# Last block's chunks before its sums, shared normalising, a third own room, and two sums moved to POOL, in an adaLN block with linear attention and an MLP

## The chip, the cores and the metric

The kernel runs on one core of one Trainium2 chip. The metric is the device time of one execution in microseconds (us); the times shown are the median of three runs, beside one profiled execution. The engines are TensorE (PE: matmuls; PEld: its weight loads), VectorE (DVE), ScalarE (ACT), GpSimd (POOL) and SyncE (SP, whose in-order queue issues all DMAs of the main loops). Each engine works through its own instructions in order and waits on semaphores of the others.

## The reference

The input has 2048 tokens of width D = 576. `mod` gives six rows of D: shift, scale and gate for attention (sa, ca, ga) and for the MLP (sb, cb, gb).

```python
mod = (silu(c) @ w_mod).reshape(1, 6, 1, D)
h = layernorm(x) * (1 + ca) + sa
q, k, v = split(h @ wqkv)                  # 32 heads of 18
pq, pk = phi(q), phi(k)                    # phi(t) = where(t > 0, t + 1, exp(t)) + 1e-6
kv = einsum("bhsd,bhse->bhde", pk, v); z = sum_s(pk)
o = (pq @ kv) / (pq . z + 1e-6)
x = x + ga * (o @ wo)
h = layernorm(x) * (1 + cb) + sb
x = x + gb * (silu(h @ w1) @ w2)           # w1: 576 x 4608, w2: 4608 x 576
```

All is float32. Every large product is made from operands split into a high part (a cast to fp32r by ACT) and a low part (the rest, a subtraction on DVE or POOL), in three passes: high by high, high by low, low by high.

## The kernel before

Tokens stand in 16 tiles of 128 (acc, four blocks of 512 tokens). A first part makes the modulation, K and V and the sums over tokens. A second part (the loop over s, up to about 405 us) runs attention's output for tile t (attn_out, L580), the layer norm of its block (stats, finish, normalise), and, per block, a generator turn_all, which transposes the normalised block (turn_chunk_k: PE transposes into a PSUM bank "small", ACT modulates it, and high and low parts go to hT). The five chunks of 128 features are 0, 2, 4, 1, 3; chunk 4 is the tail of 64 (tail_h, tail32). Beside this, the first of 18 groups of 256 hidden features is done plainly: mlp_up (L641) and mlp_down (L655), called from a list named filler.

The other 17 groups (Weights and Unit) use seven products in Winograd's manner in place of eight: the two token blocks of a pair and the feature halves make a 2x2 scheme. Their operands are sums of chunks of two blocks: turn_all makes them for the odd block of each pair (blocks 1 and 3), out of the even block's chunks, kept in h32s ("H"), and the odd block's, in temporaries "sl" (two buffers): L729 to L734 are the sums, split_s (L688 and L62) makes S. Sums for the first pair are on POOL, for the second on DVE. With two sl buffers, chunk c and chunk 2+c are turned, summed and split before the next two are turned.

The operands n = 1 to 7 of both pairs go to DRAM (hd, L685); ten of the fourteen are fetched again for every group and pair (fetch, L917), in the order ORDER = 1, 6, 2, 5, 7, 3, 4. The first two fetches have rooms of their own (rooms0, "first"); the others go in turn to three rooms: halves of h2[3] and h2[2] (both named hT) and one "room". passes(n) issues the fetch of three operands further on once its matmuls are done.

A group's weights: load1 (L871) fetches w1's columns into raw, sums1 makes four sums on POOL (L862 to L865), and up(n) splits each (L883, L62). load2 (L889) fetches w2's rows into the same single raw buffer; sums2 multiplies them by gb (L893, DVE, 128x1152), makes four sums on POOL again, and split2 splits (L905, L62).

For each unit (one group, one pair) PE alternates between Unit.up (L941), the seven up products of this unit, and the fourteen down products (L1029) of the unit before. PE's order is written by hand; that of the other engines is a planner's. After an up product DVE adds into f (L958, L965, L979), ACT takes silu (L980), and operands1 and operands2 make the down operands: ha and hb (DVE), hd, hc and he (POOL: L999, L1005, L1007, L1010, with L990 for the low half). Every down product is added on DVE (L1033) from one of four PSUM banks in two buffers, to acc or to U[b], a sum that several outputs share. In the last group add_u (L1047) adds U to three quarters of each block, and the output is stored (L1052, L1070).

The order around the change is thus set by: the hand-written order on PE, the planner's order on DVE, ACT, POOL and SP, and the rooms (single or double buffers) that DMAs and engines wait for.

Of the kernel before, what the change touches and what calls it, by code (L numbers as in the profile page):

```python
# [8 lines left out]
F32 = mybir.dt.float32  # L9
F32R = mybir.dt.float32r  # L10
# [5 lines left out]
P = 128  # L16
# [5 lines left out]
def kernel(ctx: ExitStack, tc, A_x, A_wqkv, A_wo, B_x, B_w1, B_w2, c, w_mod, out):  # L22
# [8 lines left out]
    V, A, G, T = nc.vector, nc.scalar, nc.gpsimd, nc.tensor  # L31
# [15 lines left out]
    G2 = 2  # L47
    NG = F // (G2 * P)

    def f32(ap):  # L50
        return ap.bitcast(F32)
# [9 lines left out]
    def sub_hi(lo, full, hi):  # L61
        return V.tensor_sub(lo, full, f32(hi))  # L62
# [623 lines left out]

    def split_s(S, c, t):
        A.copy(S[:, c], t)  # L688
        sub_hi(S[:, 2 + c], t, S[:, c])

    def turn_chunk_k(tb, k, h32):
        ps = small()
        transpose_chunk(xn2[tb], k, ps)
        modulate(ps, k, None, cols["b"], h32, A)
        if k < KC:
            hi, lo = hpart(tb, k, 0), hpart(tb, k, 1)
            A.copy(hi, h32)
            sub_hi(lo, h32, hi)
        else:
            tail_h(htail(tb), h32)  # L700

    def turn_all(tb):

        nonlocal wqp, h2p, tail32, h32s
        if tb == 1:
            wqp.release()
            wqp = tc.alloc_tile_pool(name="hTb", bufs=1, side="right", reuse_waits="tile")
        if tb == 3:
            pb.release()
            h2p = tc.alloc_tile_pool(name="hTc", bufs=1, side="right", reuse_waits="tile")  # L710
        h2[tb] = hTa.tile([P, 2 * KC + 2, 512], F32R, name="hT")
        pair, eng = tb // 2, (G, V)[tb // 2]
        if tb % 2 == 0:
            h32s = pc.tile([P, KC, 512], F32, name="H")
            tail32 = pc.tile([P, 512], F32, name="ht")
            for k in CHUNKS:
                turn_chunk_k(tb, k, h32s[:, k] if k < KC else tail32)
                yield
        else:
            def temp():  # L720
                return pc.tile([P, 512], F32, name="sl", bufs=2)

            pool = wqp if pair == 0 else h2p
            S = [pool.tile([P, 4, 512], F32R, name="S", bufs=2) for _ in range(2)]
# [11 lines left out]
            t = temp()  # L736
            turn_chunk_k(tb, KC, t)
            G.tensor_sub(tail32, tail32, t)
            tail_h(h2[tb - 1][:, DIFF, :], tail32)
            yield  # L740
        up, down = mlp_units(tb, w)
        if tb < NB - 1:
            filler.extend(up + down)
        else:
            filler[:] = up + filler + down
        e, o = h2[tb - tb % 2], h2[tb]
        if tb % 2 == 0:
            store_h(pair, 1, e[:, 0:4, :])
            store_h(pair, 2, e[:, 4:9, :])
        else:  # L750
            for n, q in ((0, 5), (1, 6)):
                store_h(pair, q, S[n])
            store_h(pair, 5, o[:, 9:10, :], 4)
            store_h(pair, 4, o[:, ODD : ODD + 5, :])
            store_h(pair, 3, e[:, DIFF : DIFF + 1, :], 4)
            S = [wqp.tile([P, 4, 512], F32R, name="S", bufs=2) for _ in range(2)]
            for n, q in ((0, 7), (1, 3)):
                for c in range(2):
                    split_s(S[n], c, h32s[:, 2 * n + c])
                store_h(pair, q, S[n])  # L760
                hr[q] = S[n]
                yield
# [16 lines left out]
    while s < NT + 5 or filler or turns:  # L779
        if s < QB - 2:  # L780
            filler.append(late_q)
        if s == 4:
            w = load_mlp(0)
        if NP0 <= s < NT:
            prod = pb.tile([P, D], F32, name="prod")
            G.tensor_mul(prod, acc[s], z)
            pns[s] = q_norm(s, prod, pb.tile([P, DX], F32, name="pn", bufs=2))
        t = s - 2
        if t in (5, 9, 13, 17):
            turns.append(turn_all(t // 4 - 1))  # L790
# [55 lines left out]
    class Weights:  # L846
# [43 lines left out]

        def sums2(self):
            r2, t = self.r2, self.temps(HALF)
            V.tensor_mul(r2, r2, bc["gb"].unsqueeze(1).to_broadcast([P, G2, D]))  # L893
# [18 lines left out]
    def fetch(i):  # L912
        if i < len(streamed):
            _, q, n = streamed[i]
            room = rooms0[i] if i < 2 else rooms[(i - 2) % 3]
            m = hd[q, n].shape[1]
            nc.sync.dma_start(f32(room[:, :m, :]), hd[q, n])  # L917
            in_room[i] = room

    class Unit:  # L920
# [7 lines left out]
        def passes(self, n, ps, first, k=None):  # L928

            i = at.get((self.g, self.pair, n))  # L930
            if i is None:
                h, tail = hr[n], hr_tail.get(n)
            else:
                h = in_room.pop(i)
                tail = h[:, 4, :] if k is not None else None
            w, wt = self.w.w1[n], self.w.wt
            seq = [(w[:, b], h[:, a, :]) for c in range(2) for a, b in ((c, c), (c, 2 + c), (2 + c, c))]
            if k is not None:
                seq += [(wt[:, i, k * P : (k + 1) * P], tail) for i in range(2)]
            for m, (left, right) in enumerate(seq):  # L940
                T.matmul(ps, left, right, start=first and m == 0, stop=m == len(seq) - 1, skip_group_check=True)  # L941
            if i is not None and i >= 2:
                fetch(i + 3)

        def new_f(self, i, k):
# [48 lines left out]
        def operands1(self, i):  # L994

            half = self.half
            self.split(i, "ha", half(i, 0, 0), 1)
            s3 = pf.tile([P, 1, HT], F32, name="s3")
            G.tensor_sub(s3, half(i, 0, 0), half(i, 0, 1))  # L999
            self.split(i, "hd", s3, 7, eng=G)  # L1000

        def operands2(self, i):
            half = self.half
            s = pf.tile([P, 2, HT], F32, name="s")
            G.tensor_add(s[:, 0:1], half(i, 0, 1), half(i, 1, 1))  # L1005
            self.split(i, "hb", half(i, 1, 0, 2), 2, 4)
            G.tensor_sub(s[:, 1:2], s[:, 0:1], half(i, 0, 0))  # L1007
# [64 lines left out]
    with tc.manual_schedule(engines={mybir.EngineType.PE}):  # L1072
# [82 lines left out]
```

## Time and profile before

| what | value |
|---|---|
| median of 3 runs | 1214.83 us (1214.72 to 1222.22) |
| profiled execution | 1219.38 us, span 1217.3 us |
| granted TensorE clock, mean | 0.987 |
| PE busy | 1158.2 us (95%), PEld 1052.3 us (86%) |
| DVE busy | 979.5 us (80%) |
| POOL busy | 600.3 us (49%) |
| ACT busy | 523.9 us (43%) |
| DMA | 268.59 MB, mean 221 GB/s |
| down products, L1029, and up products, L941, in the chain that ended last | 21% each |

Busy time is the time in which an engine executes; waits on semaphores are not in it. The chain that ended last is followed back from the last instruction to what released it. Durations used further on come from this one profiled execution, whose clock starts at the span's first instruction.

### The profile page before, as it was taken

Reading aid. Unit: us, or ns where it says so; the run is one execution under the profiler, and the core shown is the slowest. Engines: PE = TensorE matmul, PEld = TensorE weight load, DVE = VectorE, ACT = ScalarE, POOL = GpSimd, SP = SyncE. Lnnn points to the kernel's source line nnn. Section 1 sums busy time; section 2 is a strip of 40 time slices with the busy share of each in tenths; the row PEclk is TensorE's granted clock in tenths of the full one; section 3 lists DMA queues with packets and bytes.
Section 4 is the critical chain, followed back from the end, with each engine's and each line's share of the span. In section 5 each row is a group of like instructions: output and inputs, shape, how many; then the busy total and the mean of one; then the engine's idle time right before and its main releaser. Section 6 shows DMA issues by size and latency. Waiting matters only on the chain.

```text
span 1217.3 us, 19338 instructions
## 1 busy us (share of the span) xinstructions
PE 1158.2 (95%) x7167; PEld 1052.3 (86%) x7167; DVE 979.5 (80%) x1583; ACT 523.9 (43%) x1067; POOL 600.3 (49%) x673
## 2 busy tenths in 40 slices
PE   5999999999988899999999999999999999999997
PEld 4999999899986688889889888888888888888887
DVE  6746754898858588898888898888898888888887
ACT  5434342315546444444344444344444444444431
POOL 3200000321402376676567567657757756766761
PEclk8999999999988999999999999999999999999999
DMA  9212300213243869769679679688687687697664
GB/s 284 86 40 88 113 1 1 67 44 122 96 194 134 348 262 340 266 239 334 257 248 357 251 262 341 232 305 308 252 317 287 250 328 280 251 340 268 237 249 146
DMA packets 57579, 268.59 MB, mean 221 GB/s; under 512 B 5450, under 2 KB 20046, under 8 KB 34446
## 3 DMA queue, kind: packets, MB, share of 16 engines
q1 hardware_dynamic: 57486, 267.36, 60.4%
q8 instruction: 57, 0.93, 0.3%
q14 instruction: 36, 0.29, 0.1%
HBM read 250.56 MB, written 16.78 MB: 220 GB/s over the span
## 4 chain that ended last, share of the span: by engine, by line
PE 62%; DVE 23%; issue 6%; DMA 5%; ACT 2%; POOL 2%; SPq 0%; DVEq 0%; POOLq 0%; ACTq 0%
PE down L1029 21%; PE up L941 21%; PE psK L154 10%; DVE w L62 5%; PE big L154 4%; DVE U L1033 3%; DVE acc L1033 3%; DMA raw<-in_B_w_dram 2%; DVE raw L893 2%; DVE hb L990 2%; DVE f L979 1%; DVE ha L990 1%; PE small L641 1%; PE kvp L390 1%; DMA hT<-hd 1%
## 5 line engine op out<-in xcount | busy, mean ns | idle before, releaser
L1033 DVE TENSOR_TENSOR acc<-down,acc 128x576 f32<-128x576 f32 x335 | 245.6, 747 | 17.2 <-PE down L1029 14.2
L941 PE MATMUL up<-hT,w 128*128 128x512 f32 x876 | 227.2, 394 | 4.6 <-DMA hT<-hd 4.6
L941 PEld LDWEIGHTS up<-hT,w 128*128 128x128 f32 x876 | 156.1, 188 | 31.2 <-DVE f L979 2.8
L1005 POOL TENSOR_TENSOR s<-f,f 128x256 f32<-128x256 f32 x67 | 52.1, 778 | 244.5 <-ACT f L980 244.5
L1029 PEld LDWEIGHTS down<-w,hb 128*128 128x128 f32 x804 | 114.4, 189 | 27.7 <-DVE U L1033 14.4
L1029 PE MATMUL down<-w,hb 128*128 128x288 f32 x804 | 126.9, 300 | 11.4 <-DVE U L1033 10.5
L1033 DVE TENSOR_TENSOR U<-down,U 128x576 f32<-128x576 f32 x134 | 100.6, 751 | 39.8 <-PE down L1029 39.1
L154 PE MATMUL psK<-w,hT 128*128 128x288 f32 (+2 forms) x896 | 128.6, 302 | 1.8 <-ACT hT L133 0.9
L154 PEld LDWEIGHTS psK<-w,hT 128*128 128x128 f32 x896 | 123.8, 193 | 3.1 <-DVE hT L62 1.7
L1029 PE MATMUL down<-w,hc 128*128 128x288 f32 x804 | 122.8, 295 | 0.6 <-DVE acc L1033 0.6
L1029 PEld LDWEIGHTS down<-w,hc 128*128 128x128 f32 x804 | 116.1, 189 | 6.9 <-issue 0.8
L989 ACT CAST hc<-s 128x512 fp32r<-128x512 f32 x67 | 41.7, 622 | 135.0 <-POOL s L1007 135.0
L990 POOL TENSOR_TENSOR hc<-s,hc 128x512 fp32r<-128x512 f32 x67 | 89.2, 1331 | 11.0 <-ACT hc L989 11.0
L980 ACT ACTIVATE f<-f 128x512 f32<-128x512 f32 x102 | 64.4, 631 | 54.8 <-DVE f L979 54.5
L941 PE MATMUL up<-room,w 128*128 128x512 f32 x336 | 86.4, 392 | 0.0
L62 DVE TENSOR_TENSOR w<-raw,w 128x288 fp32r<-128x288 f32 (+2 forms) x139 | 78.1, 572 | 3.5 <-ACT w L883 3.3
L1007 POOL TENSOR_TENSOR s<-s,f 128x256 f32<-128x256 f32 x67 | 74.4, 1111 | 2.7
L1029 PE MATMUL down<-w,hd 128*128 128x288 f32 x402 | 64.5, 296 | 5.8 <-DVE acc L1033 5.8
L941 PEld LDWEIGHTS up<-room,w 128*128 128x128 f32 x336 | 59.9, 188 | 9.6
L154 PE MATMUL big<-w,qT 128*128 128x288 f32 x448 | 66.1, 301 | 2.1 <-DVE den L510 1.4
L1029 PEld LDWEIGHTS down<-w,hd 128*128 128x128 f32 x402 | 57.3, 188 | 11.6 <-ACT f L980 9.9
L941 PE MATMUL up<-hT,wt 128*128 128x512 f32 x206 | 64.7, 395 | 0.0
(220 smaller groups left out, 2369.6 us busy)
## 6 DMA issues: line engine op xcount, KB each, us to landing
hT<-hd SPq DMA_DIRECT2D x69, 1280.0 KB, 5.6
hT<-hd SPq DMA_DIRECT2D x43, 1024.0 KB, 5.9
room<-hd SPq DMA_DIRECT2D x33, 1280.0 KB, 5.7
room<-hd SPq DMA_DIRECT2D x23, 1024.0 KB, 6.4
raw<-in_B_w_dram SPq DMA_DIRECT2D x18, 576.0 KB
raw<-in_B_w_dram SPq DMA_DIRECT2D x18, 512.0 KB, 5.9
hd<-S SPq DMA_DIRECT2D x6, 1024.0 KB
xt<-in_A_x_dram SPq DMA_DIRECT2D x16, 288.0 KB, 5.3
```

The source lines that it names most:

```text
L62: return V.tensor_sub(lo, full, f32(hi))
L154: T.matmul(ps, xpart(a), wpart(b), start=n == 0, stop=n == len(XW) - 1)
L390: T.matmul(o, vt[:, j, h, :], pkt[:, :, j * HG : j * HG + P], start=(t == 0 and h == 0 and j % 2 == 0), stop=(t == NT - 1 and h == 1), ski ...
L893: V.tensor_mul(r2, r2, bc["gb"].unsqueeze(1).to_broadcast([P, G2, D]))
L941: T.matmul(ps, left, right, start=first and m == 0, stop=m == len(seq) - 1, skip_group_check=True)
L980: A.activation(f, f, AF.Silu)
L989: A.copy(t[:, :, 0, :], src)
L990: eng.tensor_sub(t[:, :, 1, :], src, f32(t[:, :, 0, :]))
L1005: G.tensor_add(s[:, 0:1], half(i, 0, 1), half(i, 1, 1))
L1007: G.tensor_sub(s[:, 1:2], s[:, 0:1], half(i, 0, 0))
L1029: T.matmul(ps[:, p, :HALF], self.a[i, n][:, u, p * P : (p + 1) * P], self.w.w2[n][:, v], start=n in (1, 5, 7, 6) and j == 0, stop=j == 2, ...
L1033: V.tensor_add(dst, ps[:, :, :HALF], dst)
```

## The change

Four things are changed.

1. In turn_all, the odd block of the second pair (block 3) turns all its five chunks first, into a tile `rows` in a room of attention's weights, and its MLP units are put into the filler list; after one yield come the sums, now two chunks wide (128x1024) in one instruction each, and the tail's. Block 1 keeps its order. split_s takes a slice of chunks, and the splits of H for S 7 and 3 are 1024 wide for both pairs.
2. Block 2's normalising is shared by ACT (tiles 1 and 3) and DVE (tiles 0 and 2), as block 3's was already; it was all on ACT.
3. Three fetches have rooms of their own, the first with place for a tail of 512 columns; the order of the three shared rooms is turned, six fetches are issued at the start instead of five, and tiles s and s3 move from pool pf to pool ph.
4. sums2's product with gb goes from DVE to POOL, for all 17 groups, and add_u from DVE to POOL, but for block 2.

In the built kernel, SP's queue holds the first load of w1's columns (L871 before, L890 after) behind the stores of block 3's S; before, it stood ahead of them.

```diff
     def split_s(S, c, t):
         A.copy(S[:, c], t)
-        sub_hi(S[:, 2 + c], t, S[:, c])
+        sub_hi(S[:, 2 + c.start : 2 + c.stop], t, S[:, c])
...
-            for c in range(2):
-                t0, t2 = temp(), temp()
-                turn_chunk_k(tb, c, t0)
-                turn_chunk_k(tb, 2 + c, t2)
+            def sums(c, t0, t2):
                 eng.tensor_sub(h32s[:, c], h32s[:, c], t0)
                 eng.tensor_add(t0, t0, t2)
                 split_s(S[0], c, t0)
                 eng.tensor_sub(t2, t2, h32s[:, c])
                 split_s(S[1], c, t2)
-                eng.tensor_sub(h32s[:, 2 + c], h32s[:, 2 + c], t2)
+                c2 = slice(2 + c.start, 2 + c.stop)
+                eng.tensor_sub(h32s[:, c2], h32s[:, c2], t2)
...
+            else:
+                rows = f32(wp.tile([P, 4, D], F32R, name="w")[:, :, :512])
+                t = temp()[:, 0]
+                for k in CHUNKS:
+                    turn_chunk_k(tb, k, rows[:, k] if k < KC else t)
+                    yield
         up, down = mlp_units(tb, w)
         if tb < NB - 1:
             filler.extend(up + down)
         else:
             filler[:] = up + filler + down
+        if tb == NB - 1:
+            yield
+            S = [h2p.tile([P, 4, 512], F32R, name="S", bufs=2) for _ in range(2)]
+            sums(slice(0, 2), rows[:, 0:2], rows[:, 2:4])
+            last_rows(t)
...
-                    lns[tb].normalise(i, xn2[tb][i], acc[4 * tb + i], A if tb < 3 or i % 2 else V)
+                    lns[tb].normalise(i, xn2[tb][i], acc[4 * tb + i], A if tb < 2 or i % 2 else V)
...
-    rooms0 = [first.tile([P, 4, 512], F32R, name=f"first{i}") for i in range(2)]
-    rooms = [h2[3][:, 0:5, :], h2[2][:, 4:9, :], rs.tile([P, 5, 512], F32R, name="room")]
+    rooms0 = {n: first.tile([P, 4 + (n == 2), 512], F32R, name=f"first{n}") for n in (2, 1, 6)}
+    rooms = [h2[2][:, 4:9, :], h2[3][:, 0:5, :], rs.tile([P, 5, 512], F32R, name="room")]
...
-            V.tensor_mul(r2, r2, bc["gb"].unsqueeze(1).to_broadcast([P, G2, D]))
+            G.tensor_mul(r2, r2, bc["gb"].unsqueeze(1).to_broadcast([P, G2, D]))
...
-            room = rooms0[i] if i < 2 else rooms[(i - 2) % 3]
+            room = rooms0[ORDER[i]] if i < 3 else rooms[i % 3]
...
-            if i is not None and i >= 2:
+            if i is not None and i >= 3:
                 fetch(i + 3)
...
-            s3 = pf.tile([P, 1, HT], F32, name="s3")
+            s3 = ph.tile([P, 1, HT], F32, name="s3")
...
-                V.tensor_add(self.c(b, i, k), self.c(b, i, k), U[b])
+                (V if self.pair == 1 and b == 2 else G).tensor_add(self.c(b, i, k), self.c(b, i, k), U[b])
...
-        for i in range(5):
+        for i in range(6):
             fetch(i)
```

More of the change, by code (lines that the diff above doesn't have):

```diff
@@ L719, in turn_all @@
         else:
[L720 to L724, printed above, removed]
-            for c in range(2):
-                t0, t2 = temp(), temp()
-                turn_chunk_k(tb, c, t0)
-                turn_chunk_k(tb, 2 + c, t2)
+            def sums(c, t0, t2):
                 eng.tensor_sub(h32s[:, c], h32s[:, c], t0)
@@ L733, in turn_all, with last_rows, temp @@
                 split_s(S[1], c, t2)
-                eng.tensor_sub(h32s[:, 2 + c], h32s[:, 2 + c], t2)
-                yield
[L736 to L740, printed above, removed]
+                c2 = slice(2 + c.start, 2 + c.stop)
+                eng.tensor_sub(h32s[:, c2], h32s[:, c2], t2)
+            def last_rows(t):
+                G.tensor_sub(tail32, tail32, t)
+                tail_h(h2[tb - 1][:, DIFF, :], tail32)
+            def temp():
+                return pc.tile([P, 1, 512], F32, name="sl", bufs=2)
+            if pair == 0:
+                S = [wqp.tile([P, 4, 512], F32R, name="S", bufs=2) for _ in range(2)]
+                for c in range(2):
+                    t0, t2 = temp(), temp()
+                    turn_chunk_k(tb, c, t0[:, 0])
+                    turn_chunk_k(tb, 2 + c, t2[:, 0])
+                    sums(slice(c, c + 1), t0, t2)
+                    yield
+                t = temp()[:, 0]
+                turn_chunk_k(tb, KC, t)
+                last_rows(t)
+                yield
+            else:
+                rows = f32(wp.tile([P, 4, D], F32R, name="w")[:, :, :512])
+                t = temp()[:, 0]
+                for k in CHUNKS:
+                    turn_chunk_k(tb, k, rows[:, k] if k < KC else t)
+                    yield
         up, down = mlp_units(tb, w)
@@ L745, in turn_all @@
             filler[:] = up + filler + down
+        if tb == NB - 1:
+            yield
+            S = [h2p.tile([P, 4, 512], F32R, name="S", bufs=2) for _ in range(2)]
+            sums(slice(0, 2), rows[:, 0:2], rows[:, 2:4])
+            last_rows(t)
         e, o = h2[tb - tb % 2], h2[tb]
@@ L757, in turn_all @@
             for n, q in ((0, 7), (1, 3)):
-                for c in range(2):
-                    split_s(S[n], c, h32s[:, 2 * n + c])
+                split_s(S[n], slice(0, 2), h32s[:, 2 * n : 2 * n + 2])
                 store_h(pair, q, S[n])
@@ L1003, in operands2 @@
             half = self.half
-            s = pf.tile([P, 2, HT], F32, name="s")
+            s = ph.tile([P, 2, HT], F32, name="s")
             G.tensor_add(s[:, 0:1], half(i, 0, 1), half(i, 1, 1))
```

## The prediction

> **What bounds the kernel now.** I read the page's slices first, then stretches with their granted clock, then the order in time of each engine where TensorE idles. The page:
>
> ```profile
> PE   5999999999988899999999999999999999999997
> ...
> PEclk8999999999988999999999999999999999999999
> ```
>
> TensorE is busy throughout, with a dent in slices 11 to 13 (335 to 426 us), where the clock falls too. The stretches (columns: us; busy us and count of PE, PEld, DVE, ACT, POOL; granted clock; DMA share; GB/s):
>
> ```profile
> 337.70:340.50 2.80, 0.00 (x0) 0.00 (x0) 0.86 (x3) 2.80 (x7) 0.00 (x0) 0.99 0.96 393
> 340.50:347.30 6.80, 5.03 (x22) 4.61 (x23) 3.08 (x5) 6.42 (x13) 0.00 (x0) 0.50 0.79 322
> ...
> 384.80:395.10 10.30, 7.58 (x17) 5.20 (x18) 8.67 (x13) 5.49 (x9) 3.11 (x5) 0.50 0.47 192
> ...
> 450.00:1171.00 721.00, 707.29 (x4125) 628.30 (x4124) 625.62 (x957) 320.82 (x692) 480.93 (x555) 1.00 0.78 287
> ```
>
> Two idles into the MLP each bring a stretch at half clock. In the long stretch PE lacks only 13.7 us. The order in time on PE (start, us, idle before it and what ended it):
>
> ```profile
> 341.87 1.11 PE L142 MATMUL small<-ident,xn 128*128 128x128 f32 x4 [4.22 <-ACT sl L643]
> ...
> 386.72 2.93 PE L641 MATMUL small<-hT,w 128*128 128x512 f32 x6 [3.68 <-ACT sl L127]
> ...
> 416.66 1.64 PE L941 MATMUL up<-hT,w 128*128 128x512 f32 x6 [2.39 <-DMA hT<-hd]
> ...
> 420.67 1.64 PE L941 MATMUL up<-hT,w 128*128 128x512 f32 x6 [1.91 <-DMA hT<-hd]
> ...
> 687.80 0.95 PE L1029 MATMUL down<-w,hc 128*128 128x288 f32 x6
> ...
> 1199.15 1.04 PE L1029 MATMUL down<-w,hd 128*128 128x288 f32 x6 [1.78 <-DVE acc L1033]
> ```
>
> So the changed places hold some 18 us of idle and slow clock; in the long stretch there is little to win and much to lose. Last, DVE and POOL around one gb product (L893), which comes every 46.6 us:
>
> ```profile
> 679.65 1.35 DVE L893 TENSOR_TENSOR raw<-raw,bc_gb 128x1152 f32<-128x1152 f32 x1
> 680.91 1.23 DVE L990 TENSOR_TENSOR hb<-f,hb 128x512 fp32r<-128x512 f32 x1
> ```
>
> ```profile
> 679.63 1.96 POOL L1007 TENSOR_TENSOR s<-s,f 128x256 f32<-128x256 f32 x1
> 682.32 1.30 POOL L990 TENSOR_TENSOR hc<-s,hc 128x512 fp32r<-128x512 f32 x1 [0.73 <-ACT hc L989]
> ```
>
> A 256-wide POOL sum takes 0.73 us elsewhere; here it takes 1.96, because it stands still while DVE reads two SBUF operands; the next hb (0.68 alone) then takes 1.23, because POOL goes on first. One of the two always waits for the other's whole instruction.
>
> **The change, part by part** (times as in the profiled execution; lines of the kernel before).
>
> *Block 2's normalising shared.* ACT's eight pieces end at 341.34 (4.47 us) and the silu that frees a PSUM bank stands behind them. Four pieces take 2.24, so the silu ends at 339.7; DVE's two tiles (1.18 each, from 2.36 for both of block 3's; the add of attention, 0.75, falls between) end at 339.9. PE resumes 2.1 us earlier. At full clock the 22 matmuls and transposes behind would save 2 us more, but an idle of 2.1 us may still halve the clock (1.78 us at 1197 was followed by 3.4 us at 0.50), and the second silu still stands behind a 1.1 us copy of S. I take -2.6, bounds -4.1 and -1.5. The Trainium skill, "TensorE: Matmul & The Clock Gate", § Why this matters for your kernels, asks for no idle over about 3 us; by that the clock would stay full and this term were -4.1. The trace's drop after 1.78 us speaks against leaning on it.
>
> *Chunks first, then sums.* The built kernel's order of instructions on each engine does put them so. Before, ACT, DVE and the two "sl" buffers alternate between chunks and sums: transposes wait, PE idles 0.88, 3.68 and 0.80, and the work at half clock costs about 3.8 (7.6 us busy at half speed). It goes from 372.0 to 404.8 with 5 transposes of 0.35, 48+48 down matmuls of 0.133 and 28 up matmuls of 0.232, 21.1 us of work. After, all five chunks stand ahead of the sums in rooms of their own, and w1's casts (2.2 us of ACT, 3 of DVE) no longer stand between. New is a wait at the end: both ups end together at about 386.6, and before the casts of hs ACT has two silus (0.6 each) and a 1024-wide cast of S (1.12): hs 2.7 us later; DVE's low half of S (1.21, between 0.68 at 512 and 1.35 at 1152) stands ahead of that of hs, another 0.5. 372.0+21.1+3.2 = 396.3 instead of 404.8.
>
> *But SP's queue is moved.* w1 was fetched at 363.4, long before its use. Now its load stands behind the stores of S, the last of which waits for DVE's sums (four of 1.21, four splits of 1.21 and the hT halves: about 390.0). Issue 390.4; landing 394.2 if the queue is free (3.8 from issue at 363.4 to ACT's cast), about 401 behind the 4.25 MB issued since 386.7 (a fetch of 1.25 and one of 1.0 that wait for the ups, two stores of 1.0) at 390 GB/s. I take 399. Cast, then the first product at 399.5 (before 405.6). The second product (6) needs POOL's third sum, 2.3 later, where the first covers 1.4: +1.0. Products 2, 5, 7, 3 find their data there: three own rooms and three reused ones are issued before; the idles of 0.28 and 2.39 go. Product 4 still waits for a room that 5 frees: issue to use 5.7 (section 6 of the page), from 406.9 to 412.6, an idle as before's 1.91. First down at 414.5 instead of 422.6. Half clock after the wait for w1: +0.7. Then POOL: the gb product (below) and four winograd sums come before hc, at about 1 us later than PE wants it. Transition from here: -6.5, bounds -11 (w1 at 394.5) and -1 (w1 at 402, two more half-clock windows).
>
> *gb on POOL, 16 times more.* No row has this operation: 128x576 takes 1.43 on POOL (L786), 128x512 1.30; doubled, less one start of 0.16, 2.7; ends 2.6 and 3.6 (twice the longest, 1.80). DVE loses 1.35. In the built order it stands between s = f+f and s -= f, so ahead of hc, s3, he and hd. r2 lands 3.7 to 5 us after its issue at 675.28, by 679.1 in most groups, so the product starts when s ends, 679.55, to 682.25. DVE's hb, due at 679.65, stands behind it to 682.9 (before 682.1); U follows at 684.8 instead of 684.6: PE +0.2. POOL: 682.25 + hb 0.6 + 0.74 + s3 0.74 + t 0.81 + 0.74 + hc 1.30, and 0.3 each for ha and two w2 splits of DVE = 688.1 to 688.7; PE wants hc's low half at 688.07 (687.80 + two matmuls). Before it was there at 683.6, so 4 us of cover are used up: +0.3. He of the second half comes at 697.7 instead of 695.0; DVE's next f waits for it and must be read before PE's up at 698.45: 0 to +0.5. Per group +0.5 in 12 groups; in the four where r2 lands late (idles of 0.93 to 1.15 behind DVE's gb product) that idle goes: -0.3. Sum +5; bounds -6 (hc in time: 13 waits of 0.17 and four of 1.0 go) and +22 (1.4 per group).
>
> *U sums.* Nine of the twelve 0.75 us adds (L1047) leave DVE; the idles of 1.04, 1.78 and 0.50 that they make in the last two units mostly go. On POOL each takes 1.43 (two rows of 288, so L786's width); two stand ahead of hc, which had 4.5 us to spare there (1175.2 against 1179.8). -2, bounds -3.3 and 0.
>
> Sum -2.6 - 6.5 + 5 - 2 = -6.1. The profiled execution took 1219.38 (span 1217.3): 1213.3. The median, 1214.83, lies 4.55 lower: **1208.7, rounded 1209**.
>
> **Rivals.** (a) *POOL becomes the bound.* If each 2.7 us product makes DVE's in-order queue wait whole and hc and he come late together, each group loses 1.4: 22-11.1 = +11, 1226: slower. It decides from hc's low half later than 688.1, which the sum above just touches. For it: POOL is busy for 16 us behind s with one gap of 0.73; against it: 7.4 us idle ahead of s, and DVE has 1.35 less. The Trainium skill, "SBUF — State Buffer", § SBUF: two separate sides, calls this pair of ports an exclusive lock, held for the whole instruction by whichever starts first; L893 and L1007 agree. (b) *POOL keeps up*: DVE's relief counts, steady -6: -17, 1198. For it: the 0.17 and 1.0 waits all follow L893. (c) *w1 late*: as at 402; transition -1 instead of -6.5, 1214. For it: no load of the trace stood behind so many stores.
>
> **How the numbers follow.** Forecast 0.52, (a) 0.17, (b) 0.18, (c) 0.13. 1% (12 us) is about what a measurement of this kernel tells from no change. Faster by more than that: (b) and a little of the forecast, 0.20; slower: over half of (a), 0.12; within, 0.68. Range: from just above (b) to the better half of (a), 1199 to 1223.
>
> **What would show it.** Right: PE's first L960 at about 397 (399.5 less 2.6), first down near 412, no 4.22 idle; w1's DMA ending the idle ahead of L960; PE waits on "hc" or POOL in the groups, period 46.6 to 47.1 us. Wrong: a period under 46.5 or over 47.6, a DMA landing at 402 or later, or idles at half clock behind 386 as long as before.

## The result, and the profile after

The changed kernel takes 1223.89 us in the median of five runs (1222.77 to 1227.59); the kernel before, beside it, 1215.83 (1214.72 to 1222.22). The ratio is 1.0064, with a 95% interval of 1.0035 to 1.0094: 8 us slower (4 to 11), where 6 us faster was forecast. The profiled execution took 1227.59 us, span 1225.9. (The "two sums" that the title has on POOL are the product with gb and the sums with U.)

To see where the 8 us come from, the span is cut at four points that every kernel here has. The **mark** is the end of the idle of 0.86 to 0.88 us that PE has ahead of a pair of tail matmuls L641, at 331.5 to 337.6 us: the work before it is the same in all kernels, but for the wider splits of block 1's S, and its time differs from execution to execution by up to 6 us. The next points are ACT's silu of f00 in the second unit and in the 33rd of 34 units, and the end of the last addition on DVE (the last stores, some 3 us, stand behind it). "One group" is the mean of the 14 groups from the fourth unit's silu to the 32nd's. All times are us, from the trace of one execution each.

| kernel | mark to last plain down | mark to first up | mark to silu, unit 2 | unit 2 to unit 33 | one group in it | unit 33 to end | mark to end |
|---|---|---|---|---|---|---|---|
| before | 71.0 | 71.9 | 97.7 | 726.9 | 46.77 | 56.0 | 880.6 |
| changed | 60.6 | 64.8 | 94.5 | 738.5 | 47.64 | 55.8 | 888.8 |

So the passage into the MLP gained 3.2 us, the long stretch lost 11.6, and the end gained 0.2: 8.2 in all.

The slices of the page (tenths of busy time of PE, and its granted clock), for the changed kernel:

```profile
PE   4999999999997899999999999999999999999997
PEclk9999999999999899999999999999999999999999
```

The dent is now two slices (the 13th and 14th) instead of three, and the clock falls in one instead of two. PE's order in time through the passage (start, us, idle before it and what ended it):

```profile
339.99 0.66 PE L142 MATMUL small<-ident,xn 128*128 128x128 f32 x4 [1.97 <-DVE st L107]
...
385.76 1.06 PE L655 MATMUL big<-w,hs 128*128 128x288 f32 x6 [2.40 <-ACT hs L644]
387.51 7.14 PE L655 MATMUL big<-w,hs 128*128 128x288 f32 x42 [0.70 <-DVE hs L62]
398.93 6.87 PE L960 MATMUL up<-first,w 128*128 128x512 f32 x18 [4.28 <-ACT w L902]
...
410.87 1.66 PE L960 MATMUL up<-room,w 128*128 128x512 f32 x6 [1.35 <-DVE f L984]
...
413.81 1.64 PE L960 MATMUL up<-hT,w 128*128 128x512 f32 x6 [0.83 <-DVE f L998]
...
421.18 1.78 PE L1048 MATMUL down<-w,hb 128*128 128x288 f32 x6 [2.30 <-DVE U L1052]
```

The idle of 4.22 us is 1.97; of the three among and behind the chunks (0.88, 3.68, 0.80) two are left, 2.40 and 0.70. New are 4.28 us for w1 and, behind it, three waits for DVE.

The long stretch (440 to 1150 us) by PE's waits (what waited, for what: us in all, times, longest). Before:

```profile
PE down L1029 <- DVE U L1033: 8.7, 25, 0.6
PE down L1029 <- DVE acc L1033: 3.6, 4, 1.0
```

Changed:

```profile
PE down L1048 <- DVE acc L1052: 19.1, 30, 0.9
PE down L1048 <- DVE U L1052: 4.7, 11, 1.2
PE up L960 <- DVE f L984: 0.5, 1, 0.5
```

24.3 us instead of 12.3, and all of it for DVE, from which 1.35 us in each group were taken away. One group shows why. POOL, then DVE, then PE, all of the changed kernel:

```profile
678.24 2.68 POOL L912 TENSOR_TENSOR raw<-raw,bc_gb 128x1152 f32<-128x1152 f32 x1
680.86 1.20 POOL L1026 TENSOR_TENSOR s<-s,f 128x256 f32<-128x256 f32 x1
...
685.39 1.28 POOL L1009 TENSOR_TENSOR hc<-s,hc 128x512 fp32r<-128x512 f32 x1
```

```profile
678.38 3.08 DVE L1009 TENSOR_TENSOR hb<-f,hb 128x512 fp32r<-128x512 f32 x1
681.39 0.68 DVE L998 TENSOR_TENSOR f<-up,p 128x512 f32<-128x512 f32 x1
681.99 0.74 DVE L1052 TENSOR_TENSOR acc<-down,acc 128x576 f32<-128x576 f32 x1
...
683.76 1.06 DVE L62 TENSOR_TENSOR w<-raw,w 128x288 fp32r<-128x288 f32 x1
684.75 0.74 DVE L1052 TENSOR_TENSOR acc<-down,acc 128x576 f32<-128x576 f32 x1
685.41 1.58 DVE L62 TENSOR_TENSOR w<-t,w 128x288 fp32r<-128x288 f32 x1
686.92 1.41 DVE L1052 TENSOR_TENSOR acc<-down,acc 128x576 f32<-128x576 f32 x2
```

```profile
682.87 1.03 PE L1048 MATMUL down<-w,hd 128*128 128x288 f32 x6 [0.37 <-DVE acc L1052]
...
687.81 1.04 PE L1048 MATMUL down<-w,hc 128*128 128x288 f32 x6 [0.93 <-DVE acc L1052]
```

DVE's hb began 0.14 us after POOL's product. It takes 0.68 us elsewhere; here 3.08, and ends 0.5 us after the product. Behind it stand, in order, adds that free PE's two down banks, and between them two splits of w2 that wait for POOL once more (1.06 and 1.58 us, 0.44 elsewhere). DVE works without a gap from 678.38 to 688.3 and comes late twice, by 0.37 and 0.93 us. In sum: DVE gave up some 24 us of product (17 x 1.41) and 6.75 us of U sums (nine of 0.75), and its busy time still rose from 979.5 to 983.4 us. Block 2's normalising brought it only 2.4 (two tiles of 1.18). So, by this sum, some 32 us of what the page counts as busy is new waiting inside instructions.

### The profile page after: what moved, and what is told of

It reads as the page before. It is cut to its first block, busy times and chain, and to the rows that moved or that the text cites. A ratio compares the mean times of both kernels' runs of the same rounds, so it can differ in the third digit from the quotient of the medians.

```text
span 1225.9 us, 19275 instructions
## 1 busy us (share of the span) xinstructions
PE 1154.5 (94%) x7167; PEld 1049.2 (86%) x7167; DVE 983.4 (80%) x1551; ACT 520.7 (42%) x1057; POOL 654.1 (53%) x699
## 4 chain that ended last, share of the span: by engine, by line
PE 53%; DVE 22%; POOL 9%; issue 9%; DMA 4%; ACT 3%; SPq 0%; POOLq 0%; ACTq 0%; DVEq 0%
PE up L960 18%; PE down L1048 17%; PE psK L154 9%; DVE w L62 4%; PE big L154 4%; DVE hb L1009 4%; DVE acc L1052 4%; DVE U L1052 3%; DMA raw<-in_B_w_dram 2%; POOL hc L1009 2%; POOL s L1018 2%; DVE f L998 1%; PE big L655 1%; PE small L641 1%; DVE hT L62 1%
## 5 line engine op out<-in xcount | busy, mean ns | idle before, releaser
L1048 PEld LDWEIGHTS down<-w,hb 128*128 128x128 f32 x804 | 114.8, 189 | 20.1 <-DVE U L1052 10.5
L62 DVE TENSOR_TENSOR w<-raw,w 128x288 fp32r<-128x288 f32 (+2 forms) x139 | 93.5, 682 | 7.9 <-ACT w L902 7.8
L1009 DVE TENSOR_TENSOR hb<-f,hb 128x512 fp32r<-128x512 f32 x68 | 83.7, 1231 | 2.1 <-ACT hb L1008 2.1
L62 DVE TENSOR_TENSOR w<-t,w 128x256 fp32r<-128x256 f32 (+1 forms) x102 | 66.7, 654 | 10.1 <-ACT w L902 9.6
L1018 POOL TENSOR_TENSOR s<-f 128x256 f32<-128x256 f32 x67 | 66.0, 985 | 13.4 <-DVE acc L1052 11.2
```

Source lines behind the costliest of these rows:

```text
L1009: eng.tensor_sub(t[:, :, 1, :], src, f32(t[:, :, 0, :]))
L1048: T.matmul(ps[:, p, :HALF], self.a[i, n][:, u, p * P : (p + 1) * P], self.w.w2[n][:, v], start=n in (1, 5, 7, 6) and j == 0, stop=j == 2, ...
```

## The experiments

The fourteen runs were made in four sets, each beside runs of the kernel before. In the tables, ratios are against those, with 95% intervals.

### First set: is it the product, and what of it?

Two edits restore what was there before, on the changed kernel. e1 has the first of them, e2 has both:

```diff
-            G.tensor_mul(r2, r2, bc["gb"].unsqueeze(1).to_broadcast([P, G2, D]))
+            V.tensor_mul(r2, r2, bc["gb"].unsqueeze(1).to_broadcast([P, G2, D]))
```

> The changed kernel with the one product by gb of each group back on DVE; everything else as changed. Theory A: the product on POOL is the whole loss of the long stretch (the same silu of a unit is 2.8 us earlier than before at 431 us and 9.5 us later at 1133 us, so some 12.3 us over 15 groups); with it gone the time is 1223.9 - 13 = 1211 (1208 to 1214), faster than before, and the period of a group is back from 47.7 to 46.6 us. Theory C, the rival: the loss comes from the rest of the change (the turned order of the rooms, s and s3 in another pool): 1222 to 1225, period still 47.7.

```diff
-                (V if self.pair == 1 and b == 2 else G).tensor_add(self.c(b, i, k), self.c(b, i, k), U[b])
+                V.tensor_add(self.c(b, i, k), self.c(b, i, k), U[b])
```

> The changed kernel with the product by gb and all sums with U back on DVE: what is left is the passage into the MLP and the rooms. The tail of the changed kernel gained 1.6 us between 1158 and 1183 us and lost 1.5 behind it, so I expect the U sums to be worth nothing: within 1.5 us of the kernel that has the product alone back, near 1211. If the U sums on POOL are worth the 2 us that I forecast, this one is 2 us slower than that one, at 1213; if its new idles of 2.65 and 1.63 us are what counts, 3 us faster, at 1208.

The product in halves, on the changed kernel:

```diff
-            G.tensor_mul(r2, r2, bc["gb"].unsqueeze(1).to_broadcast([P, G2, D]))
+            for j in range(G2):
+                G.tensor_mul(r2[:, j], r2[:, j], bc["gb"])
```

> The changed kernel with the product by gb on POOL in two instructions of 128x576 instead of one of 128x1152. Theory A1: DVE's next instruction with two SBUF operands waits for the whole POOL instruction (hb of 0.68 us took 3.08), and what it delays are DVE's adds that free PE's banks. With halves DVE gets in between them: its wait is 1.4 shorter, the loss of 13 us falls by about half, to 1217 (1214 to 1220). Theory A2: POOL's total work is the cost, and it grows by one start of some 0.1 us in each group: 1224 to 1227.

The whole product on POOL, on the kernel before:

```diff
-            V.tensor_mul(r2, r2, bc["gb"].unsqueeze(1).to_broadcast([P, G2, D]))
+            G.tensor_mul(r2, r2, bc["gb"].unsqueeze(1).to_broadcast([P, G2, D]))
```

> The kernel before with the product by gb on POOL and nothing else changed. Theory A: the loss comes with the product alone, wherever the rooms lie: 1215.8 + 13 = 1229 (1226 to 1233), period 47.4 or more. Theory C: 1216 to 1218, period 46.6 to 46.8.

| kernel | median us | ratio | mark to unit 2 | unit 2 to 33 | group | 33 to end |
|---|---|---|---|---|---|---|
| before | 1218.09 | | 97.7 | 726.9 | 46.77 | 56.0 |
| e1 product on DVE | 1209.76 | 0.9944 (0.9923 to 0.9964) | 91.8 | 723.3 | 46.56 | 56.0 |
| e2 product and U sums on DVE | 1209.61 | 0.9941 (0.9918 to 0.9963) | 93.1 | 723.4 | 46.57 | 55.7 |
| e3 product in halves on POOL | 1203.60 | 0.9883 (0.9858 to 0.9908) | 93.5 | 717.2 | 46.20 | 56.7 |
| e4 before, product on POOL | 1232.11 | 1.0113 (1.0090 to 1.0137) | 98.7 | 739.2 | 47.62 | 56.5 |

The product is the loss: the long stretch is 15.2 us longer with it on POOL than in e1, and 12.2 longer in e4 than before, with the same period. e4's group shows the same pair of instructions, on POOL and on DVE:

```profile
682.60 2.67 POOL L893 TENSOR_TENSOR raw<-raw,bc_gb 128x1152 f32<-128x1152 f32 x1
```

```profile
682.74 3.08 DVE L990 TENSOR_TENSOR hb<-f,hb 128x512 fp32r<-128x512 f32 x1
```

No gain of the U sums is seen (e1 against e2, 0.15 us by the medians and 0.3 behind unit 33), as expected from the trace and against the forecast of 2; each of the two ratios is known to some 2.5 us.

The halves did much more than expected: not half of the loss went, but all of it and 6 us more. In e3, POOL and DVE:

```profile
675.61 3.27 POOL L913 TENSOR_TENSOR raw<-raw,bc_gb 128x576 f32<-128x576 f32 x2
```

```profile
675.75 1.83 DVE L1010 TENSOR_TENSOR hb<-f,hb 128x512 fp32r<-128x512 f32 x1
```

POOL works longer (3.27 us instead of 2.68), but hb gets in between the halves and takes 1.25 us less. So it is not POOL's load (theory A2), which rose. PE's waits from 440 to 1150 us fall from 24.3 to 7.4 us, and what goes is mostly the 19.1 us for acc. The three largest that are left:

```profile
PE down L1049 <- DVE U L1053: 4.9, 14, 0.4
PE up L961 <- DVE f L985: 1.0, 1, 1.0
PE down L1049 <- DVE acc L1053: 1.0, 1, 1.0
```

One thing more is different in e3: the planner has moved DVE's second split of w2 behind the add that PE waits 0.93 us for. In the changed kernel and in e4 it stands ahead of that add. One group of e4 tells the two apart. There POOL's product began 0.24 us behind hb instead of ahead of it, whole, and with the order on DVE as in e4's other groups. POOL, then DVE:

```profile
730.74 2.99 POOL L893 TENSOR_TENSOR raw<-raw,bc_gb 128x1152 f32<-128x1152 f32 x1 [0.33 <-DVE U L1033]
```

```profile
730.50 0.68 DVE L990 TENSOR_TENSOR hb<-f,hb 128x512 fp32r<-128x512 f32 x1
...
736.80 0.51 DVE L62 TENSOR_TENSOR w<-t,w 128x288 fp32r<-128x288 f32 x1 [0.51 <-ACT w L905]
```

The second split takes 0.51 us here, not 1.58, and PE has neither of its two waits (some 0.4 and 0.9 us in most other groups). So the place of the split alone does not make them, and a whole product alone does not either; they come where hb is caught behind the product. How much the moved split adds to e3's gain was not separated.

### Second set: how short, what floor, and the passage

w1's first load ahead of the stores, on e3's kernel. The stores of S, n = 5 and 6, are kept back and bound behind the load's last DMA (tail1) in SP's order; S's pool is released behind them, and the third shared room is taken only then:

```diff
             for n, q in ((0, 5), (1, 6)):
-                store_h(pair, q, S[n])
+                if pair == 1:
+                    late.append((pair, q, S[n]))
+                else:
+                    store_h(pair, q, S[n])
...
         w.load1()
+        with tc.issue_after(w.tail1.ins):
+            for args in late:
+                store_h(*args)
...
```

> The kernel with the product in halves, and the first load of w1's columns ahead of the last block's two stores of S in SP's queue; nothing else. With halves the load is issued at 391.3 to 393.4, behind two stores of 1.0 MB, and lands at 402.7; PE has been idle since 397.4 and goes on at 402.9. Theory: the stores ahead of it are what it stands behind: it is issued 4 us earlier and has 2 MB less before it, lands before PE needs it, the idle of 5.5 us falls to under 1 us, the first up product comes 61 to 63 us after the last idle of 0.86 us (66.3 now) and the time falls by 4 (2 to 6) to about 1199.5. Rival: the next data late, the fetches of the fourth to sixth product, take its place: first down product where it is now (82.3 behind the same mark), time 1203 to 1204.

The product in quarters, on the changed kernel:

```diff
-            G.tensor_mul(r2, r2, bc["gb"].unsqueeze(1).to_broadcast([P, G2, D]))
+            for j in range(G2):
+                for k in range(2):
+                    G.tensor_mul(halves(r2[:, j])[:, k], halves(r2[:, j])[:, k], halves(bc["gb"])[:, k])
```

> The changed kernel with the product by gb on POOL in four instructions of 128x288. Halves brought the period from 47.6 to 46.2 us, below the 46.6 with the product on DVE. If what counts is only that DVE's adds reach PE's banks in time, they now do, and the wait left in each group (0.36 us behind a U add, 6 us ahead of the product) is another: 1202 to 1205, period 46.2. If the length of the lock counts in proportion, a quarter of it saves another 0.3 to 0.5 per group: 1196 to 1199, period 45.8. If POOL's load counts, three more starts of 0.1 us: 1205 to 1209.

Shared normalising alone, on the kernel before:

```diff
-                    lns[tb].normalise(i, xn2[tb][i], acc[4 * tb + i], A if tb < 3 or i % 2 else V)
+                    lns[tb].normalise(i, xn2[tb][i], acc[4 * tb + i], A if tb < 2 or i % 2 else V)
```

> The kernel before with block 2's normalising shared by ACT and DVE and nothing else changed. My term was -2.6, bounds -4.1 and -1.5. The trace of the changed kernel has the idle of 4.22 us at 1.97, with the clock full behind it, and PE 4 us earlier: by that -4 to -3.5, so some 1214 beside 1218. If the gain is lost again in the transposes that wait for the two buffers further on (idles of 0.88, 3.68 and 0.80), 0 to -1.

No product at all, on the changed kernel (in the 17 groups the output lacks the scale gb):

```diff
-            G.tensor_mul(r2, r2, bc["gb"].unsqueeze(1).to_broadcast([P, G2, D]))
```

> The changed kernel without the product of w2's rows by gb in the 17 groups (the scale is left out, so the output's MLP part lacks it). It gives the floor: neither DVE nor POOL pays. If halves on POOL are hidden in full, the period is the same 46.2 and the time 1202 to 1205. If they still cost something, the period is 45.8 or less and the time 1195 to 1199. If the loss of the changed kernel had nothing to do with the product, 1222.

| kernel | median us | ratio | mark to unit 2 | unit 2 to 33 | group | 33 to end |
|---|---|---|---|---|---|---|
| before | 1217.93 | | | | | |
| e5 halves, w1 first | 1204.94 | 0.9908 (0.9880 to 0.9936) | 89.4 | 719.5 | 46.16 | 56.2 |
| e6 quarters | 1202.96 | 0.9872 (0.9851 to 0.9892) | 94.6 | 712.9 | 45.93 | 57.3 |
| e7 before, normalising shared | 1216.10 | 0.9984 (0.9968 to 1.0001) | 95.1 | 725.3 | 46.64 | 54.9 |
| e8 no product | 1195.73 | 0.9818 (0.9798 to 0.9838) | 92.7 | 712.8 | 45.85 | 55.3 |

With quarters the long stretch is as long as without the product, 712.9 and 712.8 us, though POOL takes 3.81 us for the four. PE's waits from 440 to 1150 us in e6:

```profile
PE down L1050 <- POOL hc L1011: 1.5, 3, 0.9
PE up L962 <- DVE f L986: 0.3, 1, 0.3
```

Beside e3 it is above all the waits for U that are gone, 4.9 us in 14 groups. They lie 6 us ahead of the product, and the trace has another cause for them. In e3, ACT casts hd ahead of an operand of w1, and hd waits for POOL; the split of that operand comes late on DVE, which idles 0.78 us, and the add into U stands behind the split. ACT, then DVE, in e3:

```profile
667.37 0.41 ACT L1009 CAST hd<-s 128x256 fp32r<-128x256 f32 x1 [1.65 <-POOL s L1019]
667.68 0.40 ACT L902 CAST w<-t 128x256 fp32r<-128x256 f32 x1
```

```profile
668.12 0.90 DVE L62 TENSOR_TENSOR w<-t,w 128x256 fp32r<-128x256 f32 x1 [0.78 <-ACT w L902]
668.94 0.74 DVE L1053 TENSOR_TENSOR U<-down,U 128x576 f32<-128x576 f32 x1
```

In e6 the planner has put that cast ahead of hd's:

```profile
660.04 0.41 ACT L902 CAST w<-t 128x256 fp32r<-128x256 f32 x1 [0.23 <-PE up L962]
661.46 0.41 ACT L1010 CAST hd<-s 128x256 fp32r<-128x256 f32 x1 [1.01 <-POOL s L1020]
```

So the 4.3 us between halves and quarters in the long stretch come with another order on ACT, and no run shows that four pieces as such are better than two. By the medians the kernel without the product is still 7.2 us below the quarters. Of the 4.9 us between the two profiled executions, 0.9 lie ahead of the mark, 1.9 between it and unit 2, and 2.0 behind unit 33.

e7 is 1.8 us faster than before (between none and 4), less than the 3.5 to 4 that the changed kernel's trace let expect and more than the 0 to 1 of the other case. In its trace the last plain down comes 2.7 us earlier (68.3 from the mark), which is the forecast's term. That the clock stays full is not part of it. In e7 the idle was 2.04 us, and the 3.4 us behind it were at half clock (stretch, us, busy of PE, PEld, DVE, ACT, POOL, then granted clock):

```profile
340.30:343.70 3.40, 3.20 (x14) 3.19 (x15) 2.25 (x4) 3.03 (x6) 0.00 (x0) 0.51 1.00 414
```

e5 confirms the cause of the 4.28 us ahead of the first up product. w1's cast comes before PE needs it, and the idle is 0.90 us (PE, then ACT):

```profile
395.48 1.71 PE L963 MATMUL up<-first,w 128*128 128x512 f32 x6 [0.90 <-issue]
```

```profile
392.25 0.41 ACT L904 CAST w<-raw 128x256 fp32r<-128x256 f32 x1 [5.29 <-DMA raw<-in_B_w_dram]
```

The passage is 4.1 us shorter than e3's and 8.3 shorter than before's, yet the median is no lower than e3's, in another set. The next sets take that up.

### Third set: put together

e9 is e6's kernel with e2's edit of the U sums:

```diff
-                (V if self.pair == 1 and b == 2 else G).tensor_add(self.c(b, i, k), self.c(b, i, k), U[b])
+                V.tensor_add(self.c(b, i, k), self.c(b, i, k), U[b])
```

> Quarters on POOL, and all sums with U back on DVE. From the last silu of the next to last unit on, quarters with the U sums on POOL took 57.3 us, the kernel with both back on DVE 55.7. If the U sums cost POOL's adds in the tail what that difference says: -1.6 against quarters alone, about 1201. If they are worth nothing, as the pair with the whole product on DVE showed (1209.8 and 1209.6), 1203.

e10 is e6's kernel with e5's edit, e11 has both edits, and e12 is the kernel before with the product in quarters:

```diff
-            V.tensor_mul(r2, r2, bc["gb"].unsqueeze(1).to_broadcast([P, G2, D]))
+            for j in range(G2):
+                for k in range(2):
+                    G.tensor_mul(halves(r2[:, j])[:, k], halves(r2[:, j])[:, k], halves(bc["gb"])[:, k])
```

> Quarters on POOL, and the first load of w1 ahead of the two stores of S. With halves this brought the second unit's silu from 93.5 to 89.4 us behind the mark, and the time did not show it (1204.9 beside 1203.6, in different sets). Theory: the 4 us are real and stay: about 1199 beside 1203 for quarters. Rival: what is gained at the passage is given back in the first groups, where fetches are late (idles of 1.0 to 1.5 us at 445, 492 and 536): 1202 to 1203.

> All three: quarters on POOL, the first load of w1 ahead of the stores, the U sums on DVE. If the three add: 1203 - 4 - 1.6 = 1197.5. If the load's gain is given back: 1201. It beats the kernel before by 15 us or more either way.

> The kernel before with the product by gb on POOL in four instructions of 128x288, and nothing else changed. The whole product there cost 14 us (1232.1 beside 1218.1). If it is the length of one instruction that decides, and not where the work lies, this one is faster than before by the difference of the periods, (46.7 - 46.0) x 16 = 11 us: 1207 (1204 to 1210), period 45.9 to 46.2. If it needs the turned rooms or s and s3 in the other pool, 1214 to 1218.

| kernel | median us | ratio | mark to unit 2 | unit 2 to 33 | group |
|---|---|---|---|---|---|
| before | 1218.15 | | | | |
| e9 quarters, U sums on DVE | 1199.76 | 0.9875 (0.9843 to 0.9908) | 95.0 | 713.3 | 45.90 |
| e10 quarters, w1 first | 1243.19 | 1.0212 (1.0178 to 1.0246) | 92.3 | 756.2 | 48.39 |
| e11 quarters, w1 first, U on DVE | 1242.11 | 1.0226 (1.0192 to 1.0260) | 92.2 | 755.5 | 48.52 |
| e12 before, product in quarters | 1206.55 | 0.9914 (0.9884 to 0.9944) | 98.5 | 714.5 | 45.87 |

The same product on the same engine in the kernel before costs 14 us as one instruction (e4) and gains 11.6 as four (e12). Not all of that is the pieces': e12 has e6's order of casts on ACT too, and its waits for U are 2.8 us where e4's are 5.9; the waits for acc go from 16.9 to none. e9's ratio is e6's: no gain of the U sums is seen here either.

e10 and e11 missed all their expectations by 40 us and more, and not at the passage. PE's wait in e10, from 440 to 1150 us:

```profile
PE down L1052 <- POOL hc L1013: 29.4, 15, 2.2
```

This is the rival that the prediction called (a): hc's low half late. POOL in e10, where two more instructions than in e6 stand ahead of hc, the second sum of w2 (L884) and hd:

```profile
685.11 3.78 POOL L916 TENSOR_TENSOR raw<-raw,bc_gb 128x288 f32<-128x288 f32 x4 [7.97 <-DVE acc L1056]
688.86 0.74 POOL L1028 TENSOR_TENSOR s<-f,f 128x256 f32<-128x256 f32 x1
...
692.12 0.81 POOL L884 TENSOR_TENSOR raw<-raw 128x288 f32<-128x288 f32 x1
692.90 0.73 POOL L1013 TENSOR_TENSOR hd<-s,hd 128x256 fp32r<-128x256 f32 x1
...
694.27 1.27 POOL L1013 TENSOR_TENSOR hc<-s,hc 128x512 fp32r<-128x512 f32 x1
```

and in e6:

```profile
668.29 0.74 POOL L1026 TENSOR_TENSOR s<-f,f 128x256 f32<-128x256 f32 x1 [5.23 <-ACT f L1001]
668.99 3.81 POOL L914 TENSOR_TENSOR raw<-raw,bc_gb 128x288 f32<-128x288 f32 x4
...
675.79 1.52 POOL L1011 TENSOR_TENSOR hc<-s,hc 128x512 fp32r<-128x512 f32 x1
```

The planner orders DVE, ACT, POOL and SP anew with every edit. Counted from PE's matmuls "down hc" of the same place (666.65 in e6, 682.95 in e10), hc's low half starts after 9.1 us and after 11.3. The sum s that begins the chain to hc stands ahead of the quarters in e6 and behind them in e10, but that does not explain it, because both stand ahead of hc in both kernels. The 2.2 us are, for the most part, the two instructions (1.5 us), which in e6 stand behind hc, and a later start: POOL begins 1.6 us after those matmuls in e6 and 2.2 in e10. The waits for hc are 29.4 of the 43.3 us by which e10's long stretch is longer than e6's. The waits for U, 5.3, are back as well, and behind four of the fifteen idles for hc the granted clock was half for some 3.4 us (an estimate from that: 7 us).

### Fourth set: the order on POOL alone

The quarters are bound behind s in POOL's order, in e10's kernel (e13) and in e6's (e14). It is the s of the unit's second half, so in the trace the quarters, and w2's sums behind them, stand behind the first half's whole chain to hc (in e13 that hc starts at 676.68 and the quarters at 680.22):

```diff
+            with tc.issue_after(behind.ins) if behind else nullcontext():
                 for j in range(G2):
                     for k in range(2):
                         G.tensor_mul(halves(r2[:, j])[:, k], halves(r2[:, j])[:, k], halves(bc["gb"])[:, k])
...
-            G.tensor_add(s[:, 0:1], half(i, 0, 1), half(i, 1, 1))
+            self.s = G.tensor_add(s[:, 0:1], half(i, 0, 1), half(i, 1, 1))
...
-                    unit.w.sums2()
+                    unit.w.sums2(before and before.s)
```

> Quarters on POOL, w1's first load ahead of the two stores of S, and the quarters put behind the sum s of the unit before in POOL's order. If that order is the cause of the 1243 us, PE's waits of 1.98 us for hc go, the period is 45.9 to 46.2 us instead of 48.4, and the time is 1199 to 1203. If the load's place does it in another way, the period stays above 47.5 and the time above 1225.

> The same order on POOL, and w1's load behind the stores, as changed: 1202 to 1204, as quarters alone. The difference to e13 is what the earlier load is worth: 4 us if the idle ahead of the first up product is a true loss, 0 if the first groups give it back.

e13 takes 1203.95 us beside 1216.97 of before (ratio 0.9887, 0.9861 to 0.9913), e14 1207.27 (0.9906, 0.9881 to 0.9932). SP's order is the same in e10 and e13, so it was not the load's place nor a late fetch that made the 1243, but the order on POOL (and what the planner moved with it on DVE and ACT): e13's period is 46.47 us, and PE does not wait for hc any more:

```profile
PE down L1054 <- DVE acc L1058: 5.5, 14, 0.4
PE down L1054 <- DVE U L1058: 4.4, 11, 0.4
```

Both times lie above what was expected (1199 to 1203 and 1202 to 1204), and both kernels are slower in the long stretch (721.7 and 718.7 us) than e6 (712.9). PE has short waits for acc that e6 has not (5.5 us in e13, 5.7 in e14) and those for U again (4.4 and 3.9). The planner's order on DVE and ACT differs from e6's, and which of the differences makes the waits for acc was not tried. The earlier load gains 3.3 us by the medians (1203.95 and 1207.27); the intervals overlap, so its worth in time is not settled, though at the passage it is seen (unit 2's silu 91.8 and 99.7 us from the mark, of which e14's clock made 2).

The lowest times are those of e6 and e9, 1.3% under the kernel before. The profiled execution of e9 was the longest of its six runs (1207.64 us, with an idle of 3.14 us behind unit 33), so its end is not shown.

## Why the prediction was wrong, step by step

**Shared normalising, forecast -2.6 (-4.1 to -1.5): right.** e7 has -2.7 in its trace and -1.8 in time. The choice between the ends was the clock behind an idle of 2 us, and the runs say that it is open each time: see the last section.

**Chunks first: right.** The last plain down was forecast to end at 393.7 (396.3 less 2.6) and ended at 394.65. The two idles at the end that were forecast as 3.2 us are 2.40 and 0.70.

**w1's load: right in its place, 2 us off.** It was issued at 387.3 to 389.1 (forecast 390.4, less the 2.6 above 387.8), and the first cast of it came at 398.47 (399, less 2.6 396.4); the first up product came at 398.93 where "about 397" stood. The load took 11.2 us from its issue, not the 8.6 between 390.4 and 399. The 401 of that sum does not come out as written: 4.25 MB at 390 GB/s are 10.9 us, which from 386.7 give 397.6. That the load behind the stores is what PE waits for is shown by e5.

**The first group's products: wrong.** Forecast were waits for a DMA; the kernel waits for DVE instead (1.35, 0.83 and 2.30 us). The first of the whole products runs there too, from 407.27: DVE's ha, 0.40 us alone, takes 2.85 beside it, and DVE's f adds, for which PE waits, stand behind ha. Counted from the mark, the first up product came 7.1 us earlier than before's, where 8.7 was forecast, and the first down product 7.2 earlier (81.7 for 88.9); but from there to unit 2's silu the changed kernel takes 12.8 us, before 8.8. With the product on DVE it is 10.5 (e1) and 10.6 (e2). So of the -9.1 forecast for the passage, -3.2 came; of the 5.9 that are missing some 2.2 are the product's and 1.6 the load's, and the cause of the other 2.1 stays open. With halves and the load ahead of the stores (e5) the passage has -8.3.

**gb on POOL, forecast +5: this is the step that failed.** Measured against e1 it is +15.2 us in the long stretch, some 1.0 us in each of its 15.5 groups instead of +0.5 and -0.3. Its size was inside the bounds (-6 to +22), but the forecast put it on the wrong wait. "POOL: ... hc's low half at 688.1 to 688.7; PE wants it at 688.07" did not come about: the low half ended at 686.67, and PE, held up by the add, began on it at 687.81. "DVE's hb ... stands behind it to 682.9; PE +0.2" is where it was: the wait for the whole product was seen and worked out for hb alone, and not followed through the queue behind it, in which two splits wait for POOL again, ahead of adds that PE needs. The relief of 1.35 us was booked in DVE's favour, but a wait of 2.4 us inside hb and 1.8 inside the splits outweigh it (before, hb took 1.23, so 0.55 of waiting). With halves, the same product on POOL costs PE 1.0 us of waits for acc where the whole one costs 19.1.

The Trainium skill, "SBUF — State Buffer", § SBUF: two separate sides, says that of the two engines the one that starts first has the pair of ports "for the whole instruction; the other fully blocks". The traces agree: hb takes 3.08 us beside a product of 2.68, and 1.83 beside two halves that take 3.27 together.

**Rival (a), 1226, chance 0.17, was the nearest** in time and sign, and half of its mechanism: DVE's queue waits whole. Its point of decision, hc later than PE wants it, was not reached in the changed kernel; e10 reaches it, and there PE waits 1.98 us per group and the kernel takes 1243.

**U sums, forecast -2: none seen.** e1 and e2 differ by 0.15 us. The old idles (1.04, 1.78 and 0.50) went, and new ones of 2.65 and 1.63 us came behind POOL's he and hc, ahead of which the U sums now stand.

**Not forecast:** apart from the product the long stretch became 3.6 us shorter (e1, 723.3 against 726.9). A second trace of that stretch without any edit in it, e7's, has 725.3, so nearly half of it can be the difference of two executions; what the turned rooms did for the rest was not tried.

The sum: 5.9 us less gain at the passage, 6.6 more loss in the long stretch and 1.8 less gain at the end make the 14.3 us between -6.1 and +8.2.

## What to carry to other kernels

Work that is moved from DVE to POOL does not leave DVE if both read SBUF: the price is the length of one POOL instruction, paid by whatever DVE has in its queue behind it. So follow that queue to the bank or buffer that it frees, and cut POOL's instruction into pieces. Here the same product costs 14 us in one piece and gains 12 in four, and two pieces already took PE's waits behind it away. Where a planner orders the engines, compare the order on every engine after each edit, also an edit elsewhere, before a difference is put down to the edit: some 4 us between halves and quarters come with two casts that changed places on ACT, and e10's 40 with two POOL instructions that came to stand ahead of hc.

## What the runs showed of the hardware beyond that

- **What counts is the instruction that DVE is caught behind, not POOL's load.** POOL's time for the product of one group is 2.68 us whole, 3.27 in halves and 3.81 in quarters; PE's waits for acc from 440 to 1150 us are 19.1, 1.0 and none. The period of a group is 47.6, 46.2 and 45.9 us, and 45.85 without any product; the last step, from halves to quarters, goes with the order on ACT.
- **The clock behind an idle of 2 us is not determined by the idle.** PE's idle ahead of block 2's transposes was 1.93 to 2.04 us in thirteen executions (all kernels with shared normalising). The granted clock behind it stayed full in five of them (the changed kernel, e1, e5, e6, e9), was half for 3.4 us in six and for 6.8 us in two (e8, e14). Behind the short drop the last plain down comes hardly later (60.8 from the mark, 62.2 in e11, beside 60.6 to 60.8 with the full clock), behind the long one 2 us (62.7 and 62.9). Of e10's fifteen idles for hc, of 1.74 to 2.17 us, four were followed by half the clock. The Trainium skill, "TensorE: Matmul & The Clock Gate", § Why this matters for your kernels, warns of idle gaps over about 3 us. By these rows gaps of 2 us are already at risk.
- **A load behind stores.** w1's 512 KB and two pieces of 64 rows landed 9 to 11 us after their issue behind two stores of 1.0 MB (387.3 to 398.5 in the changed kernel, 391.3 to 402.7 in e3). In e5, issued before the stores and behind two fetches, the cast came 9.6 us after the issue, so the gain there is the earlier issue more than a faster transfer.
